# A layer norm, attention and gated feed-forward kernel: the first projections as row-half products in the written order

## The chip, the cores and the metric

The kernel runs on one core of one Trainium2 chip. The metric is the time of one execution in device microseconds; lower is better. All numbers are from one profiled execution of the kernel before, from its timed runs, or are counted in the code.

## The reference

The inputs are `x` (2048 tokens of 512) and the weights `wqkv` (512 x 1536), `wo`, `w_gate`, `w_up` (512 x 1792) and `w_down`, all in fp32. With 32 heads of 16 dimensions:

```python
xn = layernorm(x)                          # eps 1e-5, no scale, no shift
q, k, v = split(xn @ wqkv)                 # 32 heads of 16
s = softmax(q @ k.T * 16 ** -0.5) @ v      # over all 2048 keys
s = s.reshape(2048, 512) @ wo
g = silu(((xn @ w_gate) * (xn @ w_up)) @ w_down)
out = x + s * g
```

## The kernel before

**Number format.** A matrix product in fp32 is made of three products of a 32-bit format that TensorE takes at its fast rate: each operand is split into a high part (`hi`) and the rest (`lo`), and hi*hi, hi*lo and lo*hi are added up. The normed, turned tokens stand in `xh[c]` and `xl[c]`, one pair for each of four chunks `c` of 512 tokens (the pair of chunk 0 is named `fh`, `fl` in a profile). The cast and the subtraction that split a tile run on POOL, apart from chunk 0's, which ACT and DVE do.

**Units.** Attention works in 32 units of four heads by 512 queries. For each unit, scores (L837, 48 rows of the array) are reduced to their maxima by DVE (L839, tile `mx`), in 64 rounds of one matmul and one reduction. The maxima go through DRAM (`MD`) and come back as two further rows of the query tile `qs`. Then the scores are computed again, turned, with the maximum already in the sum (L865), ACT takes the exponential (L867, tile `e`), and `pv` (L876) multiplies by V. Queries and keys pass through DRAM too: a projection is split into `hl`, stored to `QD` or `KD` and loaded in another layout into `qs` or `ks`.

**Row halves.** In the main part every product but `pv` contracts over 64 or fewer rows and uses only the lower or the upper 64 rows of the array. Two such products, one in each half, run at the same time. The class `Out` is one output tile with its sums; `product(0)` issues its next lower-half product, `product(1)` its next upper-half one (L396).

**The written order.** `ORDER` is a string of 14,211 characters that `Order.run` reads; it fixes the order of PE, ACT and DVE. `o4` opens the next output in bank 4 with its first lower product, `f` is a lower and `F` an upper product, `s3` and `S3` a score for the lower or upper half into bank 3, `t` and `T` an exponential's score, `v` and `w` one and two rounds of `pv`, `e` and `d` an output's evacuation, `m` and `r` the maxima and their way through DRAM. The banks are seven PSUM banks. SP, which issues the DMAs, and POOL are put in order by the scheduler.

**The prologue.** `early()` stands ahead of that string. It loads the tokens, norms and turns chunk 0, and projects keys and queries of the first eight heads for chunk 0 (`k(0)`, `q(0)`). A loop of 265 steps then issues one full product (all 128 rows, L323) a step: V for all 16 token tiles, keys for chunks 1 to 3, queries for chunk 1. At numbers written down by hand it adds the layer norms of chunks 1 to 3 (`ln_stats`, `ln_root`, `ln_scale`, `ln_apply`), the turning of a tile (`ln_turn`, L305, four transposes of 128 x 128 into one bank, then the split), and from step 57 on, 21 groups of four scores (`EARLY`), so that 84 scores have been reduced when the written order begins.

## Time and profile before

| | |
|---|---|
| time, median of 3 runs | 1781.92 us (1779.35 to 1783.62) |
| the profiled execution's own time | 1776.43 us |
| its span (first to last instruction) | 1774.6 us |
| PE busy / DVE / ACT / POOL | 1746.1 / 1424.7 / 1232.7 / 587.9 us |
| first instruction of the written order on PE | at 113.99 us |
| last instruction of the written order on PE | at 1764.37 us |
| granted TensorE clock, mean | 0.996 |

The times are for one core. Busy times of engines overlap; a PE called busy may be running one half of its rows only, since the profile counts any matmul under way. The window 18 to 114 us is where the loop of full products runs.

### The profile page before, as it was taken

The numbers are of one execution on the slowest core, as the hardware profiler recorded it, in microseconds if no ns is written. First come the engines' busy times: TensorE is split into PE (matmuls) and PEld (weight loads), VectorE is DVE, ScalarE is ACT, GpSimd is POOL, SyncE is SP. The second block draws the span as 40 slices with busy tenths as digits, with TensorE's granted clock in tenths as the row PEclk, the third lists the DMA queues.
The fourth block names the chain that finished last, engine by engine and source line by source line (L and its number), as shares of the span: only waits on it lengthen the run. The fifth ranks groups of instructions, "written<-read, shape, count | busy, mean of one in ns | idle before, by whom it ended". The sixth has DMA issues, their size and how long they took to land.

```text
span 1774.6 us, 34733 instructions
## 1 busy us (share of the span) xinstructions
PE 1746.1 (98%) x13568; PEld 1050.1 (59%) x13568; DVE 1424.7 (80%) x2433; ACT 1232.7 (69%) x2487; POOL 587.9 (33%) x649
## 2 busy tenths in 40 slices
PE   8899999999999999999999999999999999999998
PEld 5566665556656565556665555656565655556555
DVE  7586887787888888878888888889888888889842
ACT  5236777777777777767676777776767777777783
POOL 5423233531422344233141631431334223133331
PEclk9999999999999999999999999999999999999999
DMA  5435433610213221411024221231224111111342
GB/s 203 111 97 218 167 134 112 146 46 23 76 45 74 94 76 52 76 58 44 28 64 111 82 58 29 72 75 34 90 76 100 46 37 53 40 52 58 109 139 82
DMA packets 117232, 145.77 MB, mean 82 GB/s; under 512 B 12620, under 2 KB 74060, under 8 KB 114380
## 3 DMA queue, kind: packets, MB, share of 16 engines
q1 hardware_dynamic: 117068, 143.55, 28.2%
q8 instruction: 107, 1.75, 0.4%
q14 instruction: 57, 0.47, 0.1%
HBM read 95.94 MB, written 47.45 MB: 81 GB/s over the span
## 4 chain that ended last, share of the span: by engine, by line
PE 92%; DVE 2%; DMA 2%; POOL 2%; issue 1%; ACT 0%; SPq 0%; POOLq 0%; ACTq 0%; DVEq 0%
PE b L396 33%; PE pv L876 26%; PE b L865 15%; PE b L837 14%; PE v L323 2%; DVE mx L839 1%; PE s L837 1%; DVE st L262 1%; DMA qs<-MD 1%; DMA ks<-KD 0%; POOL dl L564 0%; PE p L323 0%; DMA wdr<-in_wd_dram 0%; POOL xl L298 0%; DMA hh<-in_x_dram 0%
## 5 line engine op out<-in xcount | busy, mean ns | idle before, releaser
L839 DVE TENSOR_REDUCE mx<-b 128x1 f32<-128x512 f32 x1964 | 1218.5, 683 | 249.2 <-PE b L837 161.8
L867 ACT ACTIVATE e<-b 128x512 f32<-128x512 f32 x2048 | 1096.6, 601 | 395.4 <-PE b L865 230.2
L865 PE MATMUL b<-qs,ks 50*128 50x512 f32 x2048 | 724.8, 416 | 6.0 <-DMA qs<-MD 4.7
L837 PE MATMUL b<-ks,qs 48*128 48x512 f32 x1964 | 683.9, 415 | 0.0
L876 PE MATMUL pv<-e,V 128*32 128x512 f32 x4096 | 504.8, 600 | 0.0
L865 PEld LDWEIGHTS b<-qs,ks 50*128 50x128 f32 x2048 | 344.5, 185 | 169.2 <-ACT e L867 72.5
L837 PEld LDWEIGHTS b<-ks,qs 48*128 48x128 f32 x1964 | 330.2, 185 | 175.2 <-DVE mx L839 83.0
L876 PEld LDWEIGHTS pv<-e,V 128*32 128x32 f32 x4096 | 101.1, 109 | 214.9 <-issue 206.6
L396 PE MATMUL b<-fh,w1h 64*128 64x512 f32 x504 | 201.7, 402 | 0.3 <-ACT look L423 0.3
L396 PE MATMUL b<-fh,w0h 64*128 64x512 f32 x500 | 199.9, 403 | 0.0
L396 PE MATMUL b<-fl,w1h 64*128 64x512 f32 x504 | 198.0, 396 | 0.0
L396 PE MATMUL b<-fh,w1l 64*128 64x512 f32 x504 | 197.8, 396 | 0.0
L396 PE MATMUL b<-fl,w0h 64*128 64x512 f32 x500 | 196.7, 395 | 0.0
L396 PE MATMUL b<-fh,w0l 64*128 64x512 f32 x500 | 196.4, 396 | 0.0
L396 PE MATMUL b<-dh,hh 64*128 64x512 f32 x448 | 163.3, 400 | 0.0
L396 PE MATMUL b<-dh,hl 64*128 64x512 f32 x448 | 161.3, 396 | 0.6 <-POOL hl L366 0.6
L396 PE MATMUL b<-dl,hh 64*128 64x512 f32 x448 | 160.0, 395 | 0.0
L237 POOL CAST w0h<-w0r 128x512 fp32r<-128x512 f32 x60 | 36.6, 611 | 226.2 <-PE b L396 207.3
L396 PEld LDWEIGHTS b<-fh,w1h 64*128 64x128 f32 x504 | 92.9, 185 | 15.9 <-issue 4.4
L396 PEld LDWEIGHTS b<-fh,w1l 64*128 64x128 f32 x504 | 92.9, 186 | 15.1 <-issue 10.9
L396 PEld LDWEIGHTS b<-fh,w0l 64*128 64x128 f32 x500 | 92.5, 186 | 13.9 <-issue 9.2
L396 PEld LDWEIGHTS b<-fh,w0h 64*128 64x128 f32 x500 | 92.4, 186 | 9.4 <-issue 4.0
(165 smaller groups left out, 1947.6 us busy)
## 6 DMA issues: line engine op xcount, KB each, us to landing
w1r<-in_wg_dram SPq DMA_DIRECT2D x56, 256.0 KB
w0r<-in_wu_dram SPq DMA_DIRECT2D x56, 256.0 KB
wdr<-in_wd_dram SPq DMA_DIRECT2D x56, 256.0 KB
qs<-QD SPq DMA_DIRECT2D x64, 192.0 KB
ks<-KD SPq DMA_DIRECT2D x12, 768.0 KB
KD<-hl SPq DMA_DIRECT2D x16, 512.0 KB
QD<-hl SPq DMA_DIRECT2D x16, 512.0 KB
OD<-tr SPq DMA_DIRECT2D x31, 256.0 KB
```

The source lines that it names most:

```text
L237: cast = nc.gpsimd.tensor_copy(hi, raw)
L262: nc.vector.bn_stats(st, tokens(tt))
L323: nc.tensor.matmul(o, l(d), r(d), start=k == d == 0, stop=k == 2 and d == ND - 1)
L396: nc.tensor.matmul(self.o, l[rows], r[rows], start=x == 0 and n == 0, stop=last and (x == 0 or self.engine is not None), skip_group_check= ...
L837: nc.tensor.matmul(o, QS[i][b:b + KB, pr, t * P:(t + 1) * P], k[b:b + KB, pr, kc * 512:(kc + 1) * 512], start=True, stop=True)
L839: nc.vector.tensor_reduce(MX[i][:, j, t, kc:kc + 1], o, axis=AX.X, op=OP.max)
L865: nc.tensor.matmul(o, k[b:b + KR, pr, kt * P:(kt + 1) * P], QS[i][b:b + KR, pr], start=True, stop=True)
L867: nc.scalar.activation(e, o, AF.Exp, scale=DH ** -0.5)
L876: nc.tensor.matmul(fst["pv"][32 * j:32 * j + 32], V[:, kt, h0:h0 + 32], es[j], start=kt == 0, stop=kt == NT - 1)
```

## The change

The full products of the prologue, apart from `k(0)` and `q(0)`, become outputs of the written order: twenty `Out`s in the order of `FIRST` (`v` a token tile of V, `k` a chunk of keys, `q` the queries of chunk 1), ahead of the outputs that stood there. Each now has 12 lower and 12 upper products (L454 after). The 84 scores of `EARLY` become letters of the string (L903 after). New letters place the layer norm: `a` statistics, `g` the root, `i` the scale, `j` the normalisation of a tile, `X` the turning of two tiles, `k` the copy and split of half of what `X` wrote, `n` three memsets and loads, `u` the exponential's table.

`X` turns two token tiles in 16 transposes of 64 rows, which alternate between the lower rows into one bank and the upper rows into another. ACT then copies each bank and POOL splits it.

The string is written anew as a whole (14,980 characters). Up to a `|` in it (the first 712 characters, with all 20 new outputs opened, 224 upper products and 67 scores) SP and POOL too follow program order; after it they are scheduled as before. The numbers of products, scores and exponentials in the whole program stay the same.

SP's queue behind the loads of the tokens (`V<-in_x_dram` are the last token tiles, `w1r` and `w0r` raw projection weights, `KD_0` and `QD_0` the first chunk of keys and queries). Before:

```order
L172 DMA V<-in_x_dram 128x512 x8
L172 DMA ks_132<-ones 2x64x32
L175 DMA KD_0_60<-hl 128x1024
L175 DMA KD_0_60<-hl 128x512
L175 DMA QD_0_67<-hl 128x1024
L175 DMA QD_0_67<-hl 128x512
L175 DMA ks_132<-KD_0_60 48x2x512 x2
L175 DMA qs<-QD_0_67 48x2x512 x2
```

After:

```order
L179 DMA V<-in_x_dram 128x512 x8
L179 DMA w1r<-in_wqkv_dram 128x4x128
L179 DMA w0r<-in_wqkv_dram 128x4x128
L179 DMA w1r<-in_wqkv_dram 128x4x128
L182 DMA KD_0_60<-hl 128x1024
L182 DMA KD_0_60<-hl 128x512
L179 DMA w0r<-in_wqkv_dram 128x4x128
L182 DMA ks_132<-KD_0_60 48x2x512 x2
L182 DMA QD_0_67<-hl 128x1024
L182 DMA QD_0_67<-hl 128x512
L182 DMA qs<-QD_0_67 48x2x512 x2
```

Four loads of weights for later outputs now stand among the first keys and queries, two of them behind POOL's split of the weights before, and the store of the queries stands behind the load of the keys.

PE in the middle of the V products, before (`v_1039` is V of tile 14; `e` holds V's weights):

```order
L323 MATMUL v_1039<-e,xh_151 128x512 x8
L323 MATMUL v_1039<-e,xl_155 128x512 x2
L837 MATMUL s_2_0_1050<-ks_132,qs 128x512
L837 MATMUL s_2_1_1053<-ks_132,qs 128x512
L837 MATMUL s_2_2_1056<-ks_132,qs 128x512
L837 MATMUL s_2_3_1059<-ks_132,qs 128x512
L323 MATMUL v_1039<-e,xl_155 128x512 x2
```

After, at the first key projection of the string (`b_458` is V of tile 2, `b_521` of tile 3, `b_601` the keys of chunk 1):

```order
L454 MATMUL b_601<-xh_149,w1h 128x512
L454 MATMUL b_458<-e,fl 128x512
L454 MATMUL b_601<-xh_149,w1h 128x512
L903 MATMUL b_606<-ks_132,qs 128x512
L454 MATMUL b_601<-xh_149,w1h 128x512
L903 MATMUL b_611<-ks_132,qs 128x512
L454 MATMUL b_601<-xh_149,w1h 128x512
L454 MATMUL b_521<-e,fh 128x512
```

Lower and upper products of two outputs alternate, and a score stands singly where a half product would.

POOL around the split of the keys of chunk 1 (`hl`), before:

```order
L297 CAST xh_149<-qr 128x4x128
L298 TENSOR_TENSOR xl_153<-qr,xh_149 128x4x128
L297 CAST hl<-qr 128x512
L298 TENSOR_TENSOR hl<-qr,hl 128x512
L297 CAST xh_150<-qr 128x4x128
L298 TENSOR_TENSOR xl_154<-qr,xh_150 128x4x128
```

After:

```order
L329 CAST xh_151<-qr 128x4x2x64
L330 TENSOR_TENSOR xl_155<-qr,xh_151 128x4x2x64
L205 MEMSET V 128x8x32
L206 MEMSET V 128x8x15
L304 CAST hl<-qr 128x512
L305 TENSOR_TENSOR hl<-qr,hl 128x512
L329 CAST xh_151<-qr 128x4x2x64
```

The split of the keys of chunk 1 stood behind four splits of tokens (all of chunk 1); now it stands behind ten (chunks 1 and 2 and half of 3).

The diff, cut (of the string only the beginning is shown):

```diff
+FIRST = "vvvvkvvvkvvkqvvvvvvv"
 ORDER = """
+o0fffffffjfffjafo1lfafjX23jafFfFkafFfFfFkfFgfFfFfFio4FlfFfFfFefFfFfFfFjafFfFfFjafFX56jlao2FfFjafFfFfFkfFgfFfFfks3FiX05es6
...
-EARLY = [57, 66, 75, 84] + [98 + 10 * n for n in range(17)]
+QUEUE, SPLITS = {mybir.EngineType.SP}, {mybir.EngineType.Pool}
...
+    def ln_turn_two(tt, banks):
+        c, t = divmod(tt, 4)
+        four = lambda b, k: b.rearrange("p (d u k) -> p d u k", u=2, k=k)
+        views = [four(o, 64) for o in banks]
+        for u in range(2):
+            for d in range(ND):
+                for o, rows in zip(views, (LOWER, UPPER)):
+                    nc.tensor.transpose(o[:, d, u], tokens(tt + u)[rows, d * P:(d + 1) * P], ident[rows, rows])
+
+        def copy(half, o):
+            raw = qp.tile([P, D], F32, name="qr", bufs=3)
+            nc.scalar.activation(raw, o, AF.Copy)
...
+            nc.gpsimd.tensor_copy(hi, four(raw, 64))
+            nc.gpsimd.tensor_tensor(lo, four(raw, 64), hi, op=OP.subtract)
+        return [lambda h=h, o=o: copy(h, o) for h, o in enumerate(banks)]
...
-        yield from full(o, ((hi, lambda d: wh[d]), (hi, lambda d: wl[d]), (lo, lambda d: wh[d])))
...
+    def by_kind(kinds):
+        return [(l(d), r(d)) for l, r in kinds for d in range(ND)]
...
+        def sums():
+            hi, lo = [lambda d, x=x: x[c][:, d, sl] for x in (xh, xl)]
+            return by_kind(((hi, lambda d: wh[d]), (hi, lambda d: wl[d]), (lo, lambda d: wh[d])))
...
-            self.tpos, self.spos = [0, 0], [2 * LEAD, 2 * LEAD]
+            self.tpos, self.spos = [0, 0], [0, 0]
...
+                elif code == "X":
+                    self.todo["k"] += ln_turn_two(self.turned, [pool(int(next(codes))) for _ in range(2)])
+                    self.turned += 2
...
-        gens = [k(0), q(0), v(0, 1, 2), k(1), q(1), v(3), k(2), v(4, 5), k(3), v(*range(6, NT))]
+        stream = (n for g in (k(0), q(0)) for n in g)
...
-        order_.run(ORDER.replace("\n", ""))
+        with tc.manual_schedule(engines=QUEUE):
+            with banks_of(EARLY_BUFS):
+                ws = early()
...
+            begin, rest_of = ORDER.replace("\n", "").split("|")
+            with tc.manual_schedule(engines=SPLITS):
+                order_.run(begin)
+        order_.run(rest_of)
```

## The prediction, made before the changed kernel ran

> **What bounds the kernel now.** I read the page first: its head, the chain that ended last, and the group of DVE's reductions.

> ```profile
> span 1774.6 us, 34733 instructions
> PE 92%; DVE 2%; DMA 2%; POOL 2%; issue 1%; ACT 0%; SPq 0%; POOLq 0%; ACTq 0%; DVEq 0%
> L839 DVE TENSOR_REDUCE mx<-b 128x1 f32<-128x512 f32 x1964 | 1218.5, 683 | 249.2 <-PE b L837 161.8
> L867 ACT ACTIVATE e<-b 128x512 f32<-128x512 f32 x2048 | 1096.6, 601 | 395.4 <-PE b L865 230.2
> ```

> PE is 92% of the chain; DVE and ACT idle for 249 and 395 us, mostly until a matmul ends. PE is the bound, so PE time taken out anywhere ahead of the end is taken off the span. Next, stretches of the prologue (columns: PE, weight loads, DVE, ACT, POOL busy, granted clock, DMA share, GB/s):

> ```profile
> 20.00:40.00 20.00, 18.51 (x78) 12.40 (x77) 17.18 (x42) 12.31 (x21) 9.72 (x11) 0.91 0.31 82
> 40.00:60.00 20.00, 13.19 (x57) 9.51 (x58) 7.24 (x12) 5.23 (x9) 10.55 (x12) 0.83 0.40 119
> 36.00:38.00 2.00, 2.00 (x8) 1.50 (x7) 1.87 (x4) 1.03 (x2) 0.37 (x1) 0.51 0.00 0
> 38.00:40.00 2.00, 2.00 (x9) 1.16 (x8) 0.31 (x1) 1.45 (x3) 1.92 (x3) 0.64 0.00 0
> 54.00:56.00 2.00, 1.15 (x3) 0.70 (x4) 0.69 (x1) 0.00 (x0) 0.00 (x0) 0.50 0.89 171
> 56.00:58.00 2.00, 2.00 (x6) 1.13 (x5) 1.59 (x4) 0.00 (x0) 0.00 (x0) 0.50 0.26 40
> 58.00:60.00 2.00, 2.00 (x8) 1.63 (x7) 0.30 (x1) 0.36 (x1) 0.00 (x0) 0.52 0.00 0
> ```

> PE idles here for 8 of 40 us, and twice its clock drops to half. Then PE's timeline (start, duration, what, idle before and its releaser):

> ```profile
> 18.22 2.03 PE L323 MATMUL v<-e,fh 128*128 128x512 f32 x8
> 25.66 0.60 PE L305 MATMUL xT<-ident,ks 128*128 128x128 f32 x4
> 26.01 1.65 PE L323 MATMUL v<-e,fh 128*128 128x512 f32 x6
> 28.23 0.47 PE L837 MATMUL s<-ks,qs 48*128 48x512 f32 x1 [0.35 <-DMA qs<-QD]
> 54.52 0.76 PE L837 MATMUL s<-ks,qs 48*128 48x512 f32 x1 [6.48 <-DMA ks<-KD]
> 72.87 0.47 PE L837 MATMUL s<-ks,qs 48*128 48x512 f32 x1 [1.22 <-DMA ks<-KD]
> 105.39 0.74 PE L837 MATMUL s<-ks,qs 48*128 48x512 f32 x4
> 106.05 0.73 PE L323 MATMUL v<-e,xl 128*128 128x512 f32 x2
> 106.62 2.00 PE L323 MATMUL v<-e,xh 128*128 128x512 f32 x8
> 108.55 0.74 PE L837 MATMUL s<-ks,qs 48*128 48x512 f32 x4
> 113.99 0.50 PE L396 MATMUL b<-xh,w0h 64*128 64x512 f32 x1
> 118.54 0.62 PE L396 MATMUL b<-xh,w0h 64*128 64x512 f32 x2
> 119.71 0.62 PE L396 MATMUL b<-xh,w0l 64*128 64x512 f32 x2
> 125.16 1.92 PE L876 MATMUL pv<-e,V 128*32 128x512 f32 x16
> 127.01 0.49 PE L837 MATMUL b<-ks,qs 48*128 48x512 f32 x1
> 1764.37 0.39 PE L396 MATMUL b<-fh,w0l 64*128 64x512 f32 x1
> ```

> From it come the prices. Starts count, since matmuls overlap in the pipeline. A pair of half products costs (119.71 - 118.54) / 5 = 0.234 us. One tile's turn costs 26.01 - 25.66 = 0.35. Two rounds of `pv` cost 127.01 - 125.16 = 1.85. Ten full products and four scores cost 108.55 - 105.39 = 3.16, though as paired halves they would be 12 slots, 2.81: each change from full to half rows and back loses 0.35.

> **The window that is rewritten.** The full products of the loop run from 18.22 to 113.99, 95.8 us: 20 outputs of 12 products, 84 scores, 12 turns. As perfect pairs that is (240 + 42) x 0.234 = 66.0, and 12 x 0.35 = 4.2 for the turns: 70.2. The other 25.6 are: waits, of which 6.48, 1.22 and 0.35 are quoted, about 9.5 with four short ones of 0.3 to 0.5; half clock, (1 - 0.51) x 2 + (1 - 0.64) x 2 = 1.7 at 36 to 40 and 2.7 from 54.5 to 60; 21 changes of row mode, 21 x 0.35 = 7.4; and some 4 that I cannot place. The 6.48 is SP's doing, as its queue shows:

> ```profile
> 17.15 0.80 SPq L175 DMA_DIRECT2D KD<-hl  x2
> 20.87 1.51 SPq L175 DMA_DIRECT2D QD<-hl  x2
> 22.48 0.87 SPq L175 DMA_DIRECT2D ks<-KD  x2
> 24.83 0.78 SPq L175 DMA_DIRECT2D qs<-QD  x2
> 39.62 0.83 SPq L175 DMA_DIRECT2D KD<-hl  x2
> 49.48 0.80 SPq L175 DMA_DIRECT2D QD<-hl  x2
> 50.38 1.40 SPq L175 DMA_DIRECT2D ks<-KD  x2
> 66.15 0.81 SPq L175 DMA_DIRECT2D KD<-hl  x2
> 69.78 0.80 SPq L175 DMA_DIRECT2D ks<-KD  x2
> ```

> The keys of chunk 1 were stored at 39.62, but their load stood behind a store of queries that was not ready until 49.48. Without that, a load follows its store by 69.78 - 66.15 = 3.6, and a score follows the store by 72.87 - 66.15 = 6.7.

> **The written order after, part by part.** The string now holds 282 more lower and 282 more upper products and the same rounds of `pv`. I let everything that also stood in the old string cost what it cost, 1650.4 (113.99 to 1764.37), since waits and mode changes there are as many (319 groups of `pv` before, 321 now). What comes new ahead of it:

> 1. *Pairs.* 282 x 0.234 = 66.0. Fifteen lower products stand ahead of the first upper one and have no partner: 15 x 0.117 = 1.8.

> 2. *Turns.* Six `X` of 16 transposes. No row shows a transpose of 64 rows. One of 128 costs 0.35 / 4 = 0.088; if halves overlap in pairs an `X` takes 0.70, if each costs as much as a whole one 1.41. I take 0.8, nearer to the pairs, since half products of all other shapes overlap: 4.8 in all (4.2 to 8.4).

> 3. *The first score.* SP's queue decides it, since POOL's splits of weights and SP's loads of them now precede the first keys.

> ```profile
> 14.38 5.05 POOL L963 TENSOR_TENSOR e<-e 128x512 fp32r<-128x512 f32 x4
> 39.54 0.61 POOL L297 CAST xh<-qr 128x512 fp32r<-128x512 f32 x1
> 40.23 1.29 POOL L298 TENSOR_TENSOR xl<-qr,xh 128x512 fp32r<-128x512 f32 x1
> ```

> POOL ends V's weights at 19.43; two casts and one subtraction of the next weights end at 19.43 + 2 x 0.61 + 1.29 = 21.9. Only then can SP issue the third load of `w1r`, and behind it the store of the first keys, at 22.4 and not 17.15. The key load follows 3.6 later, 26.0, the store of the queries behind it at 26.9, the query load 24.83 - 20.87 = 3.96 later, 30.9, and the first score 28.23 - 24.83 = 3.4 later: 34.3. On PE 44 pairs' slots and two `X` precede it: 18.22 + 44 x 0.234 + 1.6 = 30.1. All later work queues behind that score: a wait of 4.2. Nothing would be lost if POOL were 4 us earlier (SP then no longer waits); if the weights land 4 us later it is 8. I take 4.0.

> 4. *Half clock.* Short waits between 28 and 35 were enough for a half clock that lost 1.7 before; the wait of 6.48 lost 2.7. For a wait of 4, I take 1.7 (0 to 4.4, both). [...]

> 5. *Later key chunks.* POOL now splits the keys of chunk 1 after ten splits of tokens. The turn behind the first score puts POOL's fifth split at about 35.9; six splits of 0.61 + 1.29, the memsets and the split of the keys end at 50.0, or 52.2 if ACT's four normalisations hold the copies up. Score 17, the first to need chunk 1, can start 6.7 later: 56.7 to 58.9. PE gets there at 34.3 + 92 x 0.234 + 4 x 0.8 + 1.7 = 60.7. So its cover is 1.8 us or more, and I cost it at 0; without cover each us of POOL is one of PE (0 to 3). Chunks 2 and 3 come out equally close by the same working.

> 6. *DVE.* Scores 41 to 115 stand beside 190 pairs and four rounds of `pv`, 48.2 us; DVE needs 74 x 0.64 (the row below) = 47.4 for them, or 50.5 at the 683 ns of the page. Its cover is thin there: 2.0 (0 to 4).

> ```profile
> 115.34 5.11 DVE L839 TENSOR_REDUCE mx<-b 128x1 f32<-128x512 f32 x8 [0.58 <-PE b L837]
> ```

> Removed and costed at nothing: the 21 changes of row mode, since the scores now stand among half products, and the 6.48, since the keys of chunk 1 no longer wait for queries.

> Sum: 66.0 + 1.8 + 4.8 + 4.0 + 1.7 + 0 + 2.0 = 80.3 in place of 95.8: 15.5 us less. The span goes from 1774.6 to 1759.1, the profiled execution's own 1776.4 to 1760.9. The median of the three runs, 1781.9, stands 5.5 above that execution; the same step from it gives 1766.4. I say 1765, somewhat nearer to the median than to the one execution.

> **The rivals.**

> *A. The exponentials hold the rest, and most of the gain is given back.* The first exponential before stands just behind 113.99; now 95 scores and four more outputs precede it, so by the same counting it starts near 109. If its cadence, not PE, set the end, only 5 us would be gained: 1777. Against it: ACT idles 395 us, 230 of them until L865 ends. 0.10.

> *B. Slower: the way of each key chunk through DRAM is laid bare.* In place of one hidden round trip there would be three, at scores 17, 33 and 49, each like the one at 54.52: 6.48 and 2.7 of half clock, 9.2 each. Term 5 has a cover of some 2 us only. The point from which it decides: two chunks fully exposed (18.4) outweigh the 15.5; three make 27.6 - 15.5 = 12 us slower, 1794. Against it: this needs POOL to be 8 us later than worked out. 0.09.

> *C. The waits vanish.* If neither the first score nor the clock loses anything and DVE keeps up, 7.7 more is gained: 1757. It needs POOL to be earlier than its row says. 0.10.

> **Chances and range.** The forecast has 0.71 (its own bounds: terms 2 to 6 at their ends give about +13 and -8). Within 0.2% (3.6 us, about what a measurement of this kernel can tell from no change) falls a part of A and of the forecast's upper end. Faster 0.83, same 0.08, slower 0.09. The range, 1752 to 1779, holds C, most of the forecast and most of A.

> **What would show it.** Right: from 18 to 90 us PE runs alternating halves at 0.234 a pair; the first score near 34 with a wait of about 4 before it on `qs<-QD`; POOL's split of the keys near 50; the letter `|` reached near 93 to 96; the first exponential near 109; behind it the same picture as before. Wrong: a wait of several us at scores 17, 33 or 49 (B); an `X` of over 1.5 us; DVE without any idle time up to 120 and PE waiting for `mx`; or a main part that takes longer than 1650 for the work it had.

## The result, and the profile after

The changed kernel takes 1761.37 us (median of four runs, 1759.58 to 1764.17), the kernel before 1782.77 us on the same chip (1779.35 to 1783.68): a ratio of 0.9885, 95% interval 0.9865 to 0.9905. The profiled execution took 1762.53 us, with a span of 1760.7 where before's was 1774.6: 13.9 us less, of the 15.5 forecast.

From the page, the head, the chain that ended last and the two busiest groups of DVE and ACT:

```profile
span 1760.7 us, 35346 instructions
PE 94%; DMA 2%; DVE 1%; POOL 1%; issue 1%; ACT 0%; SPq 0%; POOLq 0%; DVEq 0%; ACTq 0%
L905 DVE TENSOR_REDUCE mx<-b 128x1 f32<-128x512 f32 x2048 | 1264.8, 682 | 242.5 <-PE b L903 136.8
L933 ACT ACTIVATE e<-b 128x512 f32<-128x512 f32 x2048 | 1110.4, 600 | 388.1 <-PE b L931 229.4
```

PE is still the bound, and DVE and ACT still idle mostly behind a matmul. The stretches of the prologue (PE, weight loads, DVE, ACT, POOL busy, granted clock, DMA share, GB/s):

```profile
20.00:22.00 2.00, 0.00 (x0) 0.00 (x0) 1.86 (x6) 0.37 (x1) 1.76 (x4) 1.00 0.03 8
22.00:24.00 2.00, 1.75 (x6) 1.41 (x7) 1.93 (x6) 1.15 (x2) 2.00 (x2) 0.76 0.03 9
24.00:26.00 2.00, 2.00 (x6) 1.53 (x5) 1.50 (x5) 0.00 (x0) 0.06 (x1) 0.50 0.96 337
30.00:32.00 2.00, 2.00 (x12) 2.00 (x11) 1.47 (x3) 0.43 (x2) 1.92 (x3) 0.50 1.03 340
32.00:34.00 2.00, 2.00 (x15) 2.00 (x14) 1.90 (x5) 0.16 (x1) 1.72 (x2) 0.68 0.34 131
...
80.00:100.00 20.00, 19.24 (x168) 17.58 (x166) 19.36 (x34) 3.96 (x11) 2.02 (x3) 1.00 0.44 141
100.00:120.00 20.00, 20.00 (x174) 19.19 (x172) 19.21 (x34) 6.86 (x16) 8.18 (x9) 1.00 0.39 113
```

Two losses stand at the very start, and neither was in the forecast in this form: PE does nothing from 20 to 22, and then the clock is at half until past 33. DVE is full from 80 on (19.4 and 19.2 of 20 us), but PE is full beside it from 100 on. PE's timeline (start, duration, what, idle before and its releaser), then three rows of DVE, one of POOL and two of ACT:

```profile
18.02 1.07 PE L344 MATMUL p<-fl,w0h 128*128 128x512 f32 x4
22.25 3.13 PE L454 MATMUL b<-e,fh 64*128 64x512 f32 x8 [3.16 <-DVE hl L364]
33.59 1.65 PE L454 MATMUL b<-e,fh 64*128 64x512 f32 x12
35.78 0.68 PE L322 MATMUL b<-ident,ks 64*128 64x64 f32 x14
36.39 0.47 PE L454 MATMUL b<-e,fh 64*128 64x512 f32 x1
38.33 0.39 PE L903 MATMUL b<-ks,qs 48*128 48x512 f32 x1
55.45 1.42 PE L454 MATMUL b<-e,xh 64*128 64x512 f32 x9 [1.09 <-ACT look L482]
66.75 0.46 PE L903 MATMUL b<-ks,qs 48*128 48x512 f32 x1 [1.08 <-DMA ks<-KD]
```

```profile
17.17 0.66 DVE L364 TENSOR_TENSOR hl<-p,hl 128x512 fp32r<-128x512 f32 x1
17.75 1.16 DVE L274 TENSOR_SCALAR ve<-mv 128x4 f32<-128x4 f32 x1
21.52 0.68 DVE L364 TENSOR_TENSOR hl<-p,hl 128x512 fp32r<-128x512 f32 x1
55.95 1.29 POOL L305 TENSOR_TENSOR hl<-qr,hl 128x512 fp32r<-128x512 f32 x1
19.12 0.60 ACT L363 ACTIVATE hl<-p 128x512 fp32r<-128x512 f32 x1
116.57 1.25 ACT L933 ACTIVATE e<-b 128x512 f32<-128x512 f32 x2 [1.47 <-PE b L931]
```

The queries of chunk 0 are summed in a bank that the string's first output, `o0`, takes over. Their last product starts at 18.02, but DVE empties the bank only at 21.52 to 22.20, since seven small operations of a layer norm (from 17.75 on) stand before that on DVE. ACT's part of emptying it is done at 19.72, so some 1.8 of PE's wait of 3.16 us are the layer norm's (19.72 to 21.52). The string starts at 22.25 and not at 18.22. The first score starts at 38.33 and waits for nothing that the profile shows. SP's queue tells why that is no proof that its data were early:

```profile
22.84 0.37 SPq L179 DMA_DIRECT2D w1r<-in_wqkv_dram  x1
23.30 0.93 SPq L182 DMA_DIRECT2D KD<-hl  x2
24.34 0.99 SPq L179 DMA_DIRECT2D w0r<-in_wqkv_dram  x1
28.04 0.80 SPq L182 DMA_DIRECT2D ks<-KD  x2
28.89 0.90 SPq L182 DMA_DIRECT2D QD<-hl  x2
34.63 0.79 SPq L182 DMA_DIRECT2D qs<-QD  x2
57.27 0.81 SPq L182 DMA_DIRECT2D KD<-hl  x2
```

The load of the first queries was issued at 34.63; with the 3.4 us from such an issue to a score that the prediction had from before, a score could start at 38.0 (at 37.6 by the 3.0 us of the first experiment below). PE came there at 38.33. Two late chains met within 0.3 to 0.7 us: the queries through SP, and PE through the bank and the clock.

### The profile page after: what moved, and what is told of

Its sections match the earlier page's. It is cut to its first block, busy times and chain, and to the rows that moved or that the text cites. A ratio compares the mean times of both kernels' runs of the same rounds, so it can differ in the third digit from the quotient of the medians.

```text
span 1760.7 us, 35346 instructions
## 1 busy us (share of the span) xinstructions
PE 1739.2 (99%) x13856; PEld 1056.9 (60%) x13856; DVE 1420.6 (81%) x2434; ACT 1246.9 (71%) x2507; POOL 587.9 (33%) x648
## 4 chain that ended last, share of the span: by engine, by line
PE 94%; DMA 2%; DVE 1%; POOL 1%; issue 1%; ACT 0%; SPq 0%; POOLq 0%; DVEq 0%; ACTq 0%
PE b L454 36%; PE pv L942 27%; PE b L931 16%; PE b L903 15%; DMA KD<-hl 0%; DVE mx L905 0%; DMA ks<-KD 0%; DMA hh<-in_x_dram 0%; DMA ks<-in_x_dram 0%; POOL xl L330 0%; DMA wdr<-OD 0%; DVE st L269 0%; DMA wdr<-in_wo_dram 0%; POOL hl L305 0%; POOL fl L305 0%
## 5 line engine op out<-in xcount | busy, mean ns | idle before, releaser
L905 DVE TENSOR_REDUCE mx<-b 128x1 f32<-128x512 f32 x2048 | 1264.8, 682 | 242.5 <-PE b L903 136.8
L933 ACT ACTIVATE e<-b 128x512 f32<-128x512 f32 x2048 | 1110.4, 600 | 388.1 <-PE b L931 229.4
L931 PE MATMUL b<-qs,ks 50*128 50x512 f32 x2048 | 746.1, 421 | 0.4 <-ACT e L933 0.4
L903 PE MATMUL b<-ks,qs 48*128 48x512 f32 x2048 | 735.6, 415 | 2.6 <-DMA ks<-KD 1.8
L903 PEld LDWEIGHTS b<-ks,qs 48*128 48x128 f32 x2048 | 352.7, 185 | 158.7 <-DVE mx L905 73.2
L454 PE MATMUL b<-fh,w1h 64*128 64x512 f32 x504 | 200.2, 399 | 0.0
L454 PE MATMUL b<-fl,w1h 64*128 64x512 f32 x504 | 198.6, 396 | 0.0
L454 PE MATMUL b<-fh,w1l 64*128 64x512 f32 x504 | 198.2, 395 | 0.0
L454 PE MATMUL b<-fh,w0h 64*128 64x512 f32 x500 | 197.9, 397 | 0.0
L454 PE MATMUL b<-fh,w0l 64*128 64x512 f32 x500 | 197.0, 396 | 0.0
L454 PE MATMUL b<-fl,w0h 64*128 64x512 f32 x500 | 196.8, 396 | 0.0
L454 PE MATMUL b<-dh,hh 64*128 64x512 f32 x448 | 162.0, 400 | 0.0
L454 PE MATMUL b<-dl,hh 64*128 64x512 f32 x448 | 160.9, 397 | 0.0
L454 PE MATMUL b<-dh,hl 64*128 64x512 f32 x448 | 158.6, 396 | 1.7 <-POOL hl L424 1.7
L454 PEld LDWEIGHTS b<-fh,w1l 64*128 64x128 f32 x504 | 93.2, 185 | 11.8 <-issue 7.5
L454 PEld LDWEIGHTS b<-fh,w1h 64*128 64x128 f32 x504 | 93.2, 185 | 11.4 <-issue 5.0
L454 PEld LDWEIGHTS b<-fh,w0l 64*128 64x128 f32 x500 | 92.4, 185 | 11.2 <-issue 6.7
L454 PEld LDWEIGHTS b<-fh,w0h 64*128 64x128 f32 x500 | 92.5, 186 | 9.9 <-ACT e L933 1.7
```

The lines of the kernel that those rows point to most:

```text
L454: nc.tensor.matmul(self.o, l[rows], r[rows], start=x == 0 and n == 0, stop=last and (x == 0 or self.engine is not None), skip_group_check= ...
L903: nc.tensor.matmul(o, QS[i][b:b + KB, pr, t * P:(t + 1) * P], k[b:b + KB, pr, kc * 512:(kc + 1) * 512], start=True, stop=True)
L905: nc.vector.tensor_reduce(MX[i][:, j, t, kc:kc + 1], o, axis=AX.X, op=OP.max)
L931: nc.tensor.matmul(o, k[b:b + KR, pr, kt * P:(kt + 1) * P], QS[i][b:b + KR, pr], start=True, stop=True)
L933: nc.scalar.activation(e, o, AF.Exp, scale=DH ** -0.5)
```

## The experiments

**Theory T** after the comparison: the bank's wait and the half clock behind it delay PE, the weights' place in SP's queue delays the queries, and either covers the other. Taking away one gives nothing, taking away both gives 5 to 8 us. The rivals: the bank alone (R1), the queue alone (R2), or neither, since something later holds (R3). R4: the written order on SP and POOL is itself worth much. (As the expectations have them word for word below.) Four runs on one chip (before there: 1781.22).

**1. The bank alone.**

```diff
-            yield from qk_proj(wq, 0, 0, c, "x")
+            yield from qk_proj(wq, 0, 0, c, "f")
```

> The changed kernel with one word changed: the queries of chunk 0 are summed in a bank of the other early tag, so that the first output of the string no longer opens in the bank that DVE still reads at 22.2. Theory T (two chains meet at the first score: PE gets there at 38.3, its query rows land at about 38.0): the string begins near 19.0 and not at 22.25, PE stands before the first score near 30.5 and waits some 7 us for the queries; the end moves by 0 to +3 us against the changed kernel's 1761.4. Rival R1 (the bank's wait of 3.2 us and the half clock behind it, about 4.6, are the cost by themselves): 3 to 8 us faster, 1753 to 1758.

1762.16 us, ratio 0.9893 (0.9879 to 0.9907). PE's timeline of this kernel:

```profile
18.90 2.13 PE L454 MATMUL b<-e,fh 64*128 64x512 f32 x8
38.90 0.76 PE L903 MATMUL b<-ks,qs 48*128 48x512 f32 x1 [5.88 <-DMA qs<-QD]
```

The string starts 3.3 us earlier and at full clock (1.00 from 18 to 36), and all of it is lost in front of the first score, which now waits 5.88 us for the queries. It starts at 38.90, later than in the changed kernel, since the keys' trip from store to load took 7.07 us in this execution (issued at 23.27 and 30.34; 4.74 in the changed kernel). R1 falls.

**2. The weights alone.** The loads of the next two weights are held until ACT has begun to empty the first key projection of chunk 1:

```diff
-        dma(raw, src.rearrange("(d p) f -> p d f", p=P))
+        put = nc.sync.dma_start(raw, src.rearrange("(d p) f -> p d f", p=P))
+        if after is not None:
+            tc.add_manual_dep(put.ins, after, BEHIND, reason="behind the first keys and queries")
...
+            if which and c == 1:
+                fst["k1"] = first.ins.name
```

> The changed kernel with the next projection's weight loads held back behind the evacuation of the first key projection, so that SP stores and loads the first keys and queries without waiting for POOL's split of weights. Theory T: the first score's queries are there near 30, but PE still arrives at 38.3 because of the bank's wait and the half clock: within 2 us of 1761.4. Rival R2 (SP's queue is the cost, as the prediction had it): 4 to 6 us faster, 1755 to 1757.

1765.00 us, ratio 0.9901 (0.9886 to 0.9917). The queries' load is issued at 28.51 and not at 34.63. PE, and two windows of this kernel:

```profile
22.47 2.36 PE L458 MATMUL b<-e,fh 64*128 64x512 f32 x8 [1.55 <-DVE hl L366]
```

```profile
24.00:24.50 0.50, 0.50 (x3) 0.45 (x2) 0.50 (x2) 0.00 (x0) 0.00 (x0) 0.70 0.81 180
31.00:31.50 0.50, 0.50 (x7) 0.50 (x6) 0.47 (x2) 0.00 (x0) 0.50 (x2) 0.98 0.70 262
```

PE still stands behind the bank and comes to the first score at 36.99, when the queries have long been there. R2 falls too. The windows date the half clock: in half a microsecond at 0.70, 0.30 us were at half, so it begins at 24.20; by 0.98 it ends at 31.02. That is 6.82 us. This execution was also at half clock for 3.41 us ahead of the string (13.96 to 17.37), which the changed kernel's was not, and again from 89.05. So PE's own work for the queries ended later here, and the wait for the bank looks shorter (1.55).

**3. Both edits.**

> Both edits, bank and held loads. Theory T: only together do they move the first score, to about 30.5 to 31, with full clock: 5 to 8 us faster than the changed kernel, 1753.5 to 1756.5. Rivals R1 and R2: no more than the one that helped alone. A third possibility, R3: POOL's splits of tokens and the keys of chunk 1 (split ends at 57.2) hold the following scores, and only 0 to 2 us come out at the end.

1756.66 us, ratio 0.9863 (0.9849 to 0.9877): 5.5 us under the first edit and 8.3 under the second, on the same chip. PE and ACT:

```profile
31.10 1.20 PE L458 MATMUL b<-e,fh 64*128 64x512 f32 x8 [1.25 <-ACT look L486]
32.13 0.39 PE L907 MATMUL b<-ks,qs 48*128 48x512 f32 x1
...
112.09 1.22 ACT L937 ACTIVATE e<-b 128x512 f32<-128x512 f32 x2 [1.50 <-PE b L935]
```

The clock stays at 1.00 from 18 to 120 us, the first score starts at 32.13 (6.2 us earlier), the first exponential 4.5 us earlier, and the span is 5.5 shorter. T holds. Against the changed kernel's 1761.4, measured on another chip, it is 4.7 less, a little under the 5 to 8. Some of the 6.2 is given back on the way: PE waits 2.3 us for ACT's one-element reads that free the upper halves, where it was 1.1, and 2.6 for keys where it was 1.8.

**4. No written order on SP and POOL.** Both queues are left to the scheduler:

```diff
-        with tc.manual_schedule(engines=QUEUE):
+        if True:
...
-            with tc.manual_schedule(engines=SPLITS):
+            if True:
```

> The changed kernel with SP and POOL put in order by the scheduler in the prologue too, as before the change; everything else is the change's. In its listing the stores of the first keys and queries come ahead of the weight loads. Theory T (row halves in the written order carry the gain, program order little): within 2 us of 1761.4. Rival R4 (program order carries the 6.5 us wait for the keys of chunk 1 that was in the kernel before): 5 to 9 us slower, 1766 to 1770.

1765.37 us, ratio 0.9913 (0.9897 to 0.9929), between the two expectations. The queries' load is issued at 25.07 and not at 34.63, yet PE comes to the first score 16.06 us behind the string's start, as in the changed kernel (16.08): early queries alone gain nothing, as in experiment 2. The loss is later. From the waits of PE up to 125 us (in total, times, longest):

```profile
PE b L903 <- DMA ks<-KD: 4.8, 3, 2.6
```

Keys cost 4.8 us where the changed kernel loses 1.8, and the clock drops to half twice around those waits (at 66.06 and 89.95). On POOL the splits of two weights (63.3 to 67.1) now stand ahead of the key split of chunk 2, which starts at 67.11 and not at 65.01. So the written order holds up the first queries, which PE's own lateness hides, and it earns something at the keys.

**Three prices and parts by themselves** (one chip, before there 1779.86). Theory M is that the prediction's prices hold.

**5. Whole turns.** `X` as eight transposes of 128 rows in place of sixteen of 64 (the copies behind it changed to match):

```diff
-                for o, rows in zip(views, (LOWER, UPPER)):
-                    nc.tensor.transpose(o[:, d, u], tokens(tt + u)[rows, d * P:(d + 1) * P], ident[rows, rows])
+                nc.tensor.transpose(banks[u][:, d * P:(d + 1) * P], tokens(tt + u)[:, d * P:(d + 1) * P], ident)
```

> The changed kernel with X turning its two tiles by eight transposes of all 128 rows, one bank per tile, and copies and splits by tile; the order of everything else is the same. The six X of the changed kernel take about 0.6 us each in the trace. Theory M (a change between half and whole rows costs 0.35 us there and back, as the kernel before showed around its groups of four scores): an X takes 0.70 + 0.35, 2.7 us slower in all at most, less where PE waits anyway: 0 to +3 us. Rival (no price for the change of rows): +0.6 at most.

1762.98 us, ratio 0.9907 (0.9890 to 0.9923): the time can't tell it from the changed kernel. The timeline can:

```profile
36.19 1.10 PE L321 MATMUL b<-ident,ks 128*128 128x128 f32 x8
37.21 0.50 PE L451 MATMUL b<-e,fh 64*128 64x512 f32 x1
```

A whole `X` takes 1.02 us from start to start, one in halves 0.61 (36.39 - 35.78 above). Eight transposes at the prediction's 0.088 are 0.70; the other 0.32 I put down to the change of row mode and back. Halves save 0.4 us an `X`, 2.4 in all, in a part of the program that waited anyway.

**6. Before, with SP in the order of the program.**

```diff
-        with banks_of(EARLY_BUFS):
+        with banks_of(EARLY_BUFS), tc.manual_schedule(engines={mybir.EngineType.SP}):
```

> The kernel before with SP alone in program order in its prologue; full products, loop and POOL as before. Theory: the load of the keys of chunk 1 no longer stands behind the store of queries, so the wait of 6.5 us and the 2.7 of half clock behind it go, but the first score comes some 6 us later, since weight loads stand ahead of the first keys here too: 0 to 9 us faster than the kernel before, most likely 3 (1780). Rival (the order of SP is worth nothing by itself): the same as before within 1 us.

1779.05 us, ratio 0.9998 (0.9986 to 1.0009): nothing. The reason stands in the queue and on PE:

```profile
22.41 0.37 SPq L172 DMA_DIRECT2D w1r<-in_wqkv_dram  x1
22.87 0.93 SPq L175 DMA_DIRECT2D KD<-hl  x2
```

```profile
36.54 2.06 PE L837 MATMUL s<-ks,qs 48*128 48x512 f32 x4 [8.33 <-DMA qs<-QD]
```

The wait of 6.48 at 54.5 is gone, and one of 8.33 stands in front of the first score instead: the keys' store moved from 17.15 to 22.87, behind the third weight load. Program order on SP moves the loss and does not remove it.

**7. Before, with 21 more changes of row mode.** Groups of four scores between full products cut into twos:

```diff
-            if n in EARLY:
-                for _ in range(4):
+            if n in EARLY or n - 5 in EARLY:
+                for _ in range(2):
```

> The kernel before with each group of four scores in its prologue cut into two groups of two, five steps apart: 21 more changes between full and half rows, the same work. Theory M: 0.35 us each, +7.4 us (5 to 9), 1788 to 1792. Rival (the scores' own latency, not the change of rows, makes a group cost 0.35 us more): the same within 1 us.

1783.91 us, ratio 1.0032 (1.0015 to 1.0048): 5.7 us more by the ratio (4.1 by the medians), 0.27 us for each change and back (0.13 to 0.41 by the interval). The 0.35 of the prediction lies inside, so the 21 that the change removes were worth about 5.7 of its gain.

**Three on the clock and on POOL** (one chip, before there 1778.82).

**8. The gap filled.** On the second kernel (weights held):

```diff
+        filler = psum("f", "filler")
+        for _ in range(7):
+            nc.tensor.matmul(filler, wq[0][:, 0], xh[0][:, 0], start=True, stop=True)
```

> The kernel with the held weight loads (e2), and seven more full products of keys' weights by tokens, whose result nobody reads, on PE between the queries of chunk 0 and the string, so that PE does not stand idle from 20.9 to 22.5. Theory C: the clock is decided in stretches of about 3.4 us (half clock lasted 10.1 us in the changed kernel, 6.9 with the held loads, 10.3 with the free order): a stretch that holds only idle time and half products without a partner drops it, one filled mostly with paired halves lifts it. Then nothing drops here: full clock from 18 to 36, the first score at 33.3 to 34 and not at 37.0, the first exponential near 115.5 and not 118.9, and the time about 3 us under that of e2 (ratio near 0.988). Rival: the half products without a partner drop the clock by themselves: half clock from about 24 to 31 again, the first score at 37, the time of e2 (0.990) or 0.3 more.

1761.46 us, ratio 0.9899 (0.9880 to 0.9918). The fillers ended early, and 0.96 us of idle time was left:

```profile
21.78 2.13 PE L458 MATMUL b<-e,fh 64*128 64x512 f32 x8 [0.96 <-DVE hl L366]
```

```profile
24.50:25.00 0.50, 0.50 (x4) 0.39 (x3) 0.43 (x3) 0.00 (x0) 0.00 (x0) 0.56 0.92 344
27.50:28.00 0.50, 0.50 (x5) 0.50 (x4) 0.00 (x0) 0.50 (x2) 0.20 (x1) 0.53 0.00 0
```

Half clock came all the same, but for 3.41 us (24.56 to 27.97). The first score starts at 35.33, between the two expectations. The first exponential did not come earlier, though: ACT starts it at 119.08 (118.87 in the second kernel). PE waits 4.6 us for keys on the way (3.5 there), and in both the clock drops once more between 80 and 100 (0.91 over those 20 us).

**9. Partners for the unpaired halves.** On the second kernel, the idle time left as it is:

```diff
+            if self.alone < 12:
+                self.alone += 1
+                if self.alone == 1:
+                    self.partner = pool(6)
+                l, r = o.terms[0][n]
+                nc.tensor.matmul(self.partner, l[UPPER], r[UPPER], start=True, stop=True, skip_group_check=True)
```

> The kernel with the held weight loads (e2), and beside each of the first twelve lower half products of the string, which have no partner, an upper half product of the same operands into a bank that nobody reads. The idle stretch from 20.9 to 22.5 stays. Theory C (stretches of 3.4 us, paired halves lift the clock): half clock is shorter than the 6.9 us of e2, one stretch (24.2 to 27.6) or none; the first score 1.7 or 3.4 us earlier than 37.0, and the time less by as much (ratio 0.988 to 0.989). The partners themselves cost nothing, since a pair takes as long as one half alone (0.2475 and 0.234 us). Rival: the idle time alone decides, and what runs behind it counts nothing: half clock from 24.2 to 31.0, first score at 37.0, the time of e2.

1760.76 us, ratio 0.9900 (0.9884 to 0.9916). PE, and a window of this kernel:

```profile
21.41 0.49 PE L458 MATMUL b<-e,fh 64*128 64x512 f32 x1 [2.06 <-DVE hl L366]
```

```profile
22.00:24.00 2.00, 2.00 (x20) 1.64 (x17) 1.93 (x6) 0.31 (x1) 0.00 (x0) 1.00 1.06 221
```

PE was idle for 2.06 us, longer than in either of the two before, and the clock stayed at 1.00 throughout. The profiled executions beside each other, all dated as under 2:

| kernel | idle before the string | half clock behind its start | string's start to first score |
|---|---|---|---|
| 9, weights held, partners | 2.06 | none | 12.8 (1.1 of it a wait for ACT) |
| 8, weights held, gap filled | 0.96 | 3.41 | 13.6 (0.3) |
| 2, weights held | 1.55 | 6.82 | 14.5 |
| 12, the changed kernel again | 2.48 | 6.83 | 16.5 (1.3) |
| 4, free order | 2.48 | 10.24 | 16.1 |
| the changed kernel | 3.16 | 10.24 | 16.1 |
| 5, whole turns | 2.80 | 10.24 | 17.4 |
| 3, both edits | none | none | 13.0 (1.25) |
| 1, the bank alone | none | none ahead of its wait | 20.0 (7.7) |

With the waits in brackets taken off, each further 3.41 us of half clock adds 1.3 to 1.6, near the half of it (12 lies 0.7 above that, and 5 has the slower turns in it). Behind unpaired halves alone (1, 3) the clock did not drop; behind idle time and unpaired halves it did, six times of six; behind idle time and halves with partners it did not, in one execution.

How far that is luck can be read from the starts of the half clock. Within one execution they lie whole multiples of 3.413 us apart: in the second kernel at 13.96, 24.20, 89.05 and 1625.05, which is 3, 22 and 472 times 3.413 behind the first. I assume from these starts that the same steps run on at full clock; then stretches can be laid out wherever one half clock is dated. Two of kernel 8 and one of kernel 1:

```profile
10.90:14.32 3.42, 1.86 (x12) 1.53 (x12) 3.20 (x7) 2.94 (x6) 2.68 (x4) 1.00 1.05 394
21.15:24.56 3.41, 2.78 (x12) 2.25 (x13) 3.31 (x8) 1.52 (x2) 0.00 (x0) 1.00 0.69 156
18.99:22.41 3.42, 3.42 (x15) 2.61 (x15) 3.15 (x8) 1.46 (x4) 3.18 (x4) 1.00 0.23 56
```

In the first, PE is busy for 1.86 us with work on all 128 rows, and the clock stays. In the second it is busy for 2.78 us, all of it unpaired halves, and the clock drops at its end. In the third it runs unpaired halves throughout, and the clock stays. In these three, then, 2.78 us in unpaired halves went with a drop and 1.86 us on all rows with none, and 0.63 us of idle time is what the second has and the third has not.

Ahead of the string, the same program dropped the clock in the executions of kernels 2 and 10 (behind stretches with PE busy for 1.42 and 1.38 us) and not in the nine others: in the seven of them that can be dated, PE was busy for 1.73 us or more in each stretch there. What differs is where the stretches fall. Kernel 9's execution has no half clock to date its stretches by, so its 2.06 us may have been divided between two, and that the partners kept the clock is not shown. Its three other runs were granted a mean clock of 0.996 to 0.999, the second kernel's five 0.994 to 0.996. What raises the clock again stays open: the changed kernel's two executions ran the same 26 matmuls in their second stretch at half (26.46 to 29.88 and 25.11 to 28.53), and only behind the one of experiment 12 did the clock rise.

The gain in time that was forecast against the second kernel is not shown by the ratios (0.9900 and 0.9901, taken on two chips); it is seen in the traces only.

**10. ACT's copies earlier.** Both edits, and in the string two normalisations moved behind the copies that feed POOL:

```diff
-...fFjafFfFfFjafFX56jlao2FfFjafFfFfFkfFgfFfFks3FiX05e
+...fFjafFfFfFafFX56kljkjao2FfFjafFfFfFfFgfFfFs3FiX05e
```

> Both edits together (e3), and on ACT alone another order between 28 and 33 us: the two copies of the turned tokens and the one-element read that frees the upper halves go ahead of two of the three normalisations that stood before them. Theory P: POOL's chain of splits, which runs without a gap from 32.3 to 55.4 but for 1.2, decides when the keys of chunk 1 are split. It would start near 30.2, the key split would end near 49.8 and not 51.5, the wait of 1.2 on the keys at 61.1 would fall under 0.4, the wait of 1.25 at 31.1 to about 0.5, and the time by 1 to 2 us (ratio near 0.9855). Rival: the next copies of turned tokens hold POOL up again, its gap of 1.2 at 41.2 grows to 2 or more, the key split moves only as far as PE does (0.7), the wait of 1.2 stays, and the time is within 1 us of e3.

1760.06 us, ratio 0.9892 (0.9875 to 0.9910): no better than both edits alone (0.9863), rather worse. The clock had a part in that: the profiled execution was at half from 13.33 to 16.74, ahead of the string, and once more from 85.01, and the one run with a mean clock of 1.000 took 1755.89 us, where the two such runs of both edits took 1755.64 and 1756.30. POOL and PE:

```profile
42.25 0.61 POOL L331 CAST xh<-qr 128x512 fp32r<-128x512 f32 x1 [3.13 <-ACT qr L328]
```

```profile
38.44 0.50 PE L907 MATMUL b<-ks,qs 48*128 48x512 f32 x1 [1.43 <-DVE mx L909]
```

The wait of 1.25 for ACT's read at 31 us is gone, but POOL's gap before the copies of the fourth `X` grew from 1.2 to 3.1 and PE now waits 1.43 for a maximum. The rival is right in kind: POOL's chain hangs on when PE turns the tokens, not on its own length. How much of its gap of 3.1 comes from the late start of the string here (20.57, 19.16 with both edits) is not told apart.

**Both edits and the partners, against the changed kernel on one chip** (before there 1778.38).

**11 and 12. Both edits with the partners, and the changed kernel again.**

> Both edits (e3), and the upper partners of the first twelve lower half products (e9), run on the same chip as the changed kernel. Theory: the bank, the weights' place in SP's queue and the unpaired halves are three separate losses; without all three PE keeps full clock from 18 to 80 us whatever the moment at which the string starts, the first score starts 13 us or less behind the last product of the queries of chunk 0, and the time is 4 to 6 us under that of the changed kernel on this chip. The partners are neutral beside e3, whose clock did not drop. Rival: what e3 won was the chip's scatter, or is given back at the keys of chunks 1 to 3 (waits of 2.6 us there in e3 against 1.8): within 2 us of the changed kernel.

> The changed kernel once more, unaltered, as the measure for the run with both edits on the same chip. Expected: a ratio to before of 0.987 to 0.990, a wait of about 3 us before the string's first product, half clock for about 10 us behind it, the first score 19 to 20 us behind the last product of the queries of chunk 0. If the half clock were an accident of that one execution, it would not be there or have another length.

1758.04 us, ratio 0.9888 (0.9872 to 0.9905), against 1761.67, ratio 0.9910 (0.9896 to 0.9925): 3.6 us less, under the 4 to 6 expected. The intervals of the two ratios touch, but each of the four runs (at most 1760.08) is faster than each of the changed kernel's (at least 1761.51). The traces add a span 3.1 shorter and a first exponential 4.1 earlier, at full clock, with the first score 13.0 us behind the string's start. That the partners add to both edits is not shown (0.9888 here, 0.9863 without them). The changed kernel's second execution:

```profile
20.86 3.09 PE L454 MATMUL b<-e,fh 64*128 64x512 f32 x8 [2.48 <-DVE hl L364]
37.37 0.47 PE L903 MATMUL b<-ks,qs 48*128 48x512 f32 x1 [0.94 <-PE b L454]
```

The bank's wait is there again (2.48) and half clock again, though 6.83 us of it (21.70 to 28.53). PE came to the first score earlier and stood before it for 0.94; the row names another matmul, but the queries' load was issued at 34.12, 3.25 before the score. The two chains meet again, and this time SP's is the later.

## Why the prediction was right, step by step

The time (1765 forecast, 1761.4 measured) came out for reasons that are only partly those given. The sum put the first exponential near 109; it came at 116.1 on PE, 6.4 later than its terms for the 330 pairs ahead of it give (18.22 + 77.2 + 14.3 = 109.7). What follows the first exponential then cost 4.8 us less than allowed. The two leave the span's 1.6 over the forecast; that they nearly cancel is in good part luck.

1. *Pairs.* The slot holds: twelve halves from 33.59 to 34.99 are 0.233 a pair. The unpaired ones were mis-sized. I gave them half a slot, 0.117; eight of them took 1.98 us in the first experiment (18.90 to 20.88), 0.2475 each, a whole slot. That is 1.7 more.
2. *Turns.* 0.61 where I took 0.8: 1.2 less in all. Halves do overlap: sixteen take less than the 0.70 of eight whole ones.
3. *First score.* The step that failed. A wait of 4.0 for SP was forecast, with PE there at 30.1. SP's chain was right in kind and later than worked out (queries' load at 34.63, not 30.9): its two trips through DRAM took 4.74 and 5.74 us from store to load, where 3.6 and 3.96 were taken from before. But PE was late by itself and the wait did not show. What I did not see is who frees `o0`'s bank: 4.0 us of late start (3.3 of them the bank's, since the string starts at 18.90 in the first experiment) took the place of the 4.0 us of waiting, by luck of size.
4. *Half clock.* 10.24 us at half lose 5.1, where I took 1.7 and bounded at 4.4, from two losses of the kernel before. The largest error of size, 3.4 us, and outside its own bounds. Ahead of the six half clocks behind the string's start stood idle time of 0.96 us (experiment 8) to 3.16 us (here), with unpaired halves behind it, and PE stayed at half for 10.24 us here (23.06 to 33.30) without a gap in its work.
5. *Later key chunks.* Costed at 0 (0 to 3): 1.8 us of waits on keys and 1.1 for ACT's read; with two short ones (one is the 0.4 of term 6) the waits behind the start come to 3.5. The key split of chunk 1 ended at 57.2, not at 50.0 to 52.2. It waited little only because PE was late as well. The tenth experiment shows what moves it.
6. *DVE.* 2.0 (0 to 4) forecast, 0.4 found (one wait for `mx`, before 44 us). DVE is as full as I said, yet PE has 20.0 of 20 us beside it.

So 1.7 - 1.2 + 0 + 3.4 + 3.5 - 2.0 = 5.4 of the 6.4 are placed; 1.0 is not.

*The rest of the string* did not cost the same. Before's string opened with unpaired halves too (116.66 to 117.37 in its trace: one every 0.23 or 0.24 us); they were inside the 1650.4, and term 1 counted such halves once more. Counted in halves up to the first `pv`, that gives back about 2.4 us. Another 2.5 behind it I can't assign. Of the other signs, the 67th score, the last ahead of `|`, starts at 98.52, where 93 to 96 was forecast. And the ends of terms 2 to 6 add up to +15.3, not to the +13 that stands under the chances.

The removed items: the 21 mode changes are worth 5.7 by experiment 7, against the 7.4 that I listed. The 6.48 did go, and experiments 1 and 6 show a wait of its size at the first score in its place (5.88 and 8.33) when PE is there early.

*Rival A* (the exponentials hold the rest) fell: ACT idles 388 us. *Rival B* needed 9.2 at each key chunk; there were waits of 1.08 and 0.76. *Rival C* (no waits at the first score, 1757) was not this kernel. The two edits reach its time (1756.7, and 1758.0 with the partners), though with waits left: in experiment 3 2.6 us for keys and 2.3 for ACT's reads.

## What to carry to other kernels

When a prologue becomes part of one string, look first at who empties the banks that the string's first outputs take over: an evacuation behind seven small operations of another task kept PE standing for 3.2 us here, 1.8 of them for those operations, and 10.24 us of half clock followed. When two chains end at the same instruction, removing one shows nothing; remove both before calling either harmless. And a partner for the first half products, real or idle, costs no slot (0.2475 us alone, 0.233 as a pair); full clock behind idle time, with partners, is seen in one execution.
